# Small VectorE and GpSimd steps re-sourced, and the order of a unit's VectorE steps fixed, in a delta-rule and expert-layer kernel

## The chip, the cores and the metric

The kernel runs on one core of a Trainium2 chip. The time is that of the whole program on the device, in microseconds; the kernel before has a median of 824.09 us in three runs. In the text PE is TensorE (matmuls), PEld its weight loads, DVE is VectorE, ACT is ScalarE, POOL is GpSimd, and SP is SyncE, which issues most of the DMAs here.

## The reference

32 heads (4 batches of 8) run a delta rule over 768 steps with head size 48; the 3072 rows that come out (384 wide) go through an expert layer with a rational activation.

```python
for t in range(S):
    y[:, :, t] = einsum('bhd,bhde->bhe', q[:, :, t], state)
    v_old = einsum('bhde,bhd->bhe', state, kt)           # kt: normalized key
    state = state + bt * einsum('bhd,bhe->bhde', kt, vt - v_old)
...
h = x @ w_in                                             # 384 -> 2048
P = a[0] + a[1] * h + a[2] * h**2 + a[3] * h**3
Q = 1.0 + abs(b[0]) * abs(h) + abs(b[1]) * h**2
out = (P / (Q + 1e-06)) @ w_out                          # 2048 -> 384
```

## The kernel before, in words

The 768 steps are cut into 12 chunks of 64. Within a chunk the recurrence becomes matrix work: a Gram matrix of the keys (`pg`, line 565), the inverse of a triangular system (`inverse`, lines 574 to 642, small VectorE steps on 128x256 numbers), four rounds of solving (`solve_start`, `solve_step`, `solved`: tiles `pu` and `z`), the next state (`S`, line 763), its split (`sh`, line 726) and the outputs `y`. Each chunk of outputs is 256 rows, transposed into `xT` (line 808), and the expert layer takes them in 8 units of 256 hidden columns. So there are 96 units; unit n belongs to chunk n // 8. Numbers are kept as two float16 halves, high and low, and a product is three matmul passes; `split16` (line 238) makes the halves, the high one on ACT or POOL, the low one on DVE or POOL.

One unit has five parts. `hidden` is 18 matmuls into PSUM (`ph`, two buffers). `numerator` has the three DVE steps that read `ph`, called the PSUM steps here: line 859 (u = ph u), line 861 (w = (z + B0) ph) and line 863 (u = (u + A1) ph), behind two ACT steps (lines 856 and 858), with a third ACT step in between (line 862). `quotient` takes 1/Q by a logarithm and an exponential on ACT (lines 874 and 875), and then the DVE steps that read two SBUF tiles: the high half g (line 880, or 878), the product back (line 881) and the remainder (line 885); POOL makes the low half (line 886). In chunks 2 to 10 the units 0, 4, 5 and 6 of a chunk give the addition of A0 (line 867) and the remainder (line 883) to POOL as well (`by_pool`). `accumulate` is 12 matmuls into `po`, of which only the last four read the low half. The tiles u, r and w (`mu`, `mr`, `mw`) have three buffers each.

The loop over n writes numerator(n), quotient(n-1), a slice of the attention work of later chunks, accumulate(n-2) and hidden(n+1). That is the order of the program text only: the order on each engine is made at build time by a list scheduler, by readiness in its own model of the engines and by priorities (the solves stand at raised priority). An engine then executes its list in order, so an instruction that waits holds up all behind it. `tc.issue_after(x)` puts what is written in its block behind x in the list of x's engine; it is an order, not a wait for a result.

At the start the weights, which arrive as 64-bit floats, are made into 32-bit ones by `to_f32` (line 377): 56 blocks, each a DMA of word pairs, an ACT step on the high words (line 384), a POOL step that leaves the sign (line 385) and two DVE steps that put the bits together (line 387).

Of the kernel before, what the change touches and what calls it, by code (L numbers as in the profile page):

```python
# [37 lines left out]
def kernel(  # L38
# [338 lines left out]
    def to_f32(t, src, nm, bias=BIAS):  # L377

        n = t.shape[-1]
        st = staged([P, n, 2], U32, "ws" + nm)  # L380
        nc.sync.dma_start(out=st.rearrange("p f w -> p (f w)"), in_=src)
        wl, wh = st[..., 0], st[..., 1]
        a = sb.tile([P, n], F32, tag="mg", name="wa" + nm, bufs=MB)
        nc.scalar.activation(a, wh.bitcast(F32), AF.Abs, scale=bias)
        nc.gpsimd.tensor_scalar(t.bitcast(F32), wh.bitcast(F32), 0.0, 0.0, op0=ALU.min, op1=ALU.mult)
        for word, scalar, op0 in ((wl, 29, ALU.logical_shift_right), (a.bitcast(U32), 3, ALU.logical_shift_left)):
            nc.vector.scalar_tensor_tensor(out=t, in0=word, scalar=scalar, in1=t, op0=op0, op1=ALU.bitwise_or)

# [172 lines left out]
    def key_products(c):  # L561
        d = info[c]
        gd = d["gd"] = dpool.tile([P, BS], F32, tag="gd", name=f"gd_{c}")
        pg = bank(ps_f, f"pg_{c}", C)
        mm3(pg, d["kbd"], d.pop("tk"))
        g = sb.tile([P, HP, C], F32, tag="g", name=f"g_{c}", bufs=1)
        nc.scalar.mul(by_pair(g), pg[2], -1.0)
        for b in range(2):
            nc.sync.dma_start(out=as_rows(gd, b), in_=g[b * C : (b + 1) * C])
        gl = sb.tile([P, HP, C - 16, 2], F16, tag="gl", name=f"gl_{c}", bufs=1)  # L570
        split16([gl[..., i] for i in range(2)], g[:, :, : C - 16], eng=nc.gpsimd, hi=nc.gpsimd)
        d["gl"] = gl

    def inverse(c):


        d = info[c]
        gb = sb.tile([P, 272], F32, tag="gb", name=f"gb_{c}", bufs=1)
        dma = nc.sync.dma_start(out=gb[:, :256].rearrange("p (i j) -> p i j", j=16), in_=as_blocks(d.pop("gd")))
# [12 lines left out]

        w4 = blocks(wt, 4, 0, 68)
        a4 = xt.rearrange("p (e i j) -> p e i j", e=4, i=4)
        b4 = bblk[:, c].rearrange("p (e i) -> p e i", e=4)
        nc.vector.tensor_mul(a4, blocks(gb, 4, 0, 68), b4.unsqueeze(3).broadcast_to([P, 4, 4, 4]))
        for i in range(1, 4):
            pv = pr[:, : 4 * i * i].rearrange("p (e k j) -> p e k j", e=4, k=i)
            ai = a4[:, :, i, :i].unsqueeze(2).broadcast_to([P, 4, i, i])
            nc.vector.tensor_mul(pv, w4[:, :, :i, :i], ai)  # L600
            nc.vector.tensor_reduce(w4[:, :, :i, i], pv, axis=AX.X, op=ALU.add)

        for n in (4, 8):
            x = 34 * n
            e = 8 // n
            shape = [P, n, n, n]
            w21 = blocks(wt, n, n, x)
            prod = pr[:, : e * n ** 3].rearrange("p (e a b j) -> p e a b j", e=e, a=n, b=n)
            xs = xt[:, : e * n * n].rearrange("p (e i j) -> p e i j", e=e, i=n)
            g21, w11, w22 = blocks(gb, n, 16 * n, x), blocks(wt, n, 0, x), blocks(wt, n, 17 * n, x)  # L610
            for m in range(e):
                nc.vector.tensor_mul(
                    prod[:, m], g21[:, m].unsqueeze(1).broadcast_to(shape), w11[:, m].unsqueeze(2).broadcast_to(shape)
                )
# [12 lines left out]
        wh = sb.tile([P, 256, 2], F16, tag="wh", name=f"wh_{c}", bufs=1)
        nc.vector.tensor_scalar_mul(wh[..., 0], wtf, 256.0)
        nc.vector.scalar_tensor_tensor(
            out=wh[..., 1], in0=wtf, scalar=256.0, in1=wh[..., 0], op0=ALU.mult, op1=ALU.subtract  # L630
        )
        if c == 0:
            nc.vector.tensor_scalar(
                gate.bitcast(U32), wtf[:, 127:128].bitcast(U32), 0, 15 << 23, op0=ALU.bitwise_and, op1=ALU.bitwise_or
            )
        im = img[c % NIMG]
        words = wh.rearrange("p x i -> p (x i)").bitcast(F32)
        nc.sync.dma_start(out=as_blocks(im), in_=words.rearrange("m (t c) -> m t c", c=16))
        wc = d["wc"] = sb.tile([P, HP, C, 2], F16, tag="wc", name=f"wc_{c}", bufs=1)
        words = wc.rearrange("p m s i -> p (m s i)").bitcast(F32).rearrange("p (m s) -> p m s", s=C)  # L640
        for b in range(2):
            nc.sync.dma_start(out=words[b * C : (b + 1) * C], in_=as_rows(im, b))
# [138 lines left out]
    def tokens(c):  # L781
        yt = ys.pop(c)
        pool = ps_c if c < 3 else ps_f
        x = sb.tile([P, 2, NCC, TG], F16, tag="xT", name=f"xT_{c}")
        xs = sb.tile([P, 2], F32, tag="xs", name=f"xs_{c}")
        xm, fs = (xs[:, i : i + 1] for i in range(2))
        hot = sb.tile([P, 1], BF16, tag="hx", name=f"hx_{c}")
        sf = sb.tile([P, 6], F32, tag="sf", name=f"sf_{c}", bufs=3)
        sx = sf[:, 2:3]

        sum_squares(fs, yt.rearrange("p a e -> p (a e)"), x[:, 0].rearrange("p c t -> p (c t)"))
        px = pool.tile([P, NPAIR * 512], F32, tag="a", name=f"px_{c}")
# [12 lines left out]
        for p in PAIRS:
            for cc in range(NCC):
                nc.tensor.transpose(px[:, cc, p * P : (p + 1) * P], yt[:, p, cc * P : (cc + 1) * P], identf)
        split16(parts(x), px, sx)
        toks[c] = {"x": x, "sf": sf, "hot": hot, "ikap": {}}

    def scalars(c, lo, hi):

# [36 lines left out]
    def numerator(n):  # L849
# [6 lines left out]
        nc.scalar.activation(u, ph, AF.Identity, scale=A3, bias=a2)  # L856
        r = z = sb.tile([P, 2, TG], F32, tag="mr", name=f"mr{n}", bufs=MB)
        nc.scalar.activation(z, ph, AF.Abs, scale=B1)  # L858
        nc.vector.tensor_mul(u, ph, u)  # L859
        w = sb.tile([P, 2, TG], F32, tag="mw", name=f"mw{n}", bufs=MB)  # L860
        nc.vector.scalar_tensor_tensor(out=w, in0=z, scalar=B0, in1=ph, op0=ALU.add, op1=ALU.mult)  # L861
        nc.scalar.activation(w, w, AF.Abs)  # L862
        nc.vector.scalar_tensor_tensor(out=u, in0=u, scalar=A1, in1=ph, op0=ALU.add, op1=ALU.mult)  # L863
# [6 lines left out]
    def quotient(n):  # L870
# [3 lines left out]
        nc.scalar.activation(r, w, AF.Ln, bias=Q0)  # L874
        nc.scalar.activation(r, r, AF.Exp, scale=-1.0)  # L875
        g = sb.tile([P, 2, 2, TG], F16, tag="mg", name=f"mg{n}", bufs=MB)
        if by_pool:
            nc.vector.tensor_mul(g[:, 0], u, r)  # L878
        else:
            nc.vector.scalar_tensor_tensor(out=g[:, 0], in0=u, scalar=A0, in1=r, op0=ALU.add, op1=ALU.mult)  # L880
        nc.vector.scalar_tensor_tensor(out=w, in0=w, scalar=Q0, in1=g[:, 0], op0=ALU.add, op1=ALU.mult)  # L881
        if by_pool:
            nc.gpsimd.tensor_sub(u, u, w)  # L883
        else:
            nc.vector.scalar_tensor_tensor(out=u, in0=u, scalar=A0, in1=w, op0=ALU.add, op1=ALU.subtract)  # L885
        nc.gpsimd.tensor_mul(g[:, 1], u, r)  # L886
        d["g"] = g

# [38 lines left out]
    def back(c, j):  # L927
# [19 lines left out]
            outputs(c)  # L947
        elif j == 6:
            tokens(c)
        elif j == 7:  # L950
            if c > 0:
                scalars(c, 0, NU)

    def front(c, j):

# [123 lines left out]
```

## Time and profile before

| | |
|---|---|
| median of 3 runs (lowest, highest) | 824.09 us (821.0, 824.83) |
| the profiled execution: its time, its span | 823.32 us, 821.6 us |
| mean granted TensorE clock in it | 0.946 |
| first PSUM step of unit 0, of unit 48 | 140.7 us, 468.5 us |

The span runs from the first to the last instruction; 1.7 us of the execution lie around it. A group's row gives line, engine, operation, tiles written and read, shapes and count, then the busy time in us, the mean in ns, and the idle time ahead of it with what ended it. Durations on DVE include about 60 ns in which the next instruction already runs, so their sum is a little over the engine's busy time.

### The profile page before, as it was taken

To read this page: it belongs to the slowest core of one execution; us is meant where nothing else is said; L and a number is where in the kernel's file an instruction comes from. 1 tells how busy PE (TensorE), PEld (TensorE's weight loads), DVE (VectorE), ACT (ScalarE), POOL (GpSimd) and SP (SyncE) were. 2 spreads that over 40 slices of the span, in tenths; PEclk is the share of its full clock that TensorE was granted. 3 is DMA by queue.
4 is the path that set the end of the run, shared out by engine and by line. 5 is a ranking of instruction groups with operands and counts; after the bars stand their busy time and mean duration, and the time that the engine had idled before them with its cause. 6 is when DMAs were issued, how large, how long until landed. Compare 5 with 4: busy or idle time off the path is not lost.

```text
span 821.6 us, 23603 instructions
## 1 busy us (share of the span) xinstructions
PE 644.8 (78%) x9642; PEld 518.6 (63%) x9642; DVE 738.5 (90%) x1268; ACT 576.8 (70%) x1008; POOL 463.0 (56%) x415
## 2 busy tenths in 40 slices
PE   1321456688988889898897888988989988999995
PEld 0211355567766767776685776776777866887663
DVE  4898888798899999799899889898999799998996
ACT  3767767567867776778678578668578746877773
POOL 8987965534553473746835736635846446353532
PEclk9999856888999999999999999998999999999999
DMA  8988755728655666674565365554473632400000
GB/s 229 214 197 212 163 105 100 129 43 157 97 92 102 116 97 121 104 141 88 105 129 92 64 124 86 98 109 85 74 136 55 116 57 57 78 2 21 2 20 19
DMA packets 361100, 82.91 MB, mean 101 GB/s; under 512 B 350496, under 2 KB 357664, under 8 KB 360992
## 3 DMA queue, kind: packets, MB, share of 16 engines
q1 hardware_dynamic: 358816, 80.25, 51.6%
q8 instruction: 75, 1.23, 0.6%
q10 hardware_dynamic: 2176, 1.17, 0.5%
q14 instruction: 33, 0.27, 0.1%
HBM read 34.70 MB, written 13.65 MB: 59 GB/s over the span
## 4 chain that ended last, share of the span: by engine, by line
DVE 41%; PE 22%; DMA 10%; issue 8%; ACT 8%; POOL 6%; SPq 3%; POOLq 0%; DVEq 0%; ACTq 0%
PE ph L839 7%; PE po L901 6%; DVE mw L881 4%; DVE mu L859 4%; DVE mw L861 4%; DVE mu L863 4%; DVE mg L880 3%; DVE mu L885 3%; DVE mg L878 2%; DVE z L249 2%; PE pu L463 2%; POOL mg L886 2%; PE py L463 2%; DMA gb<-gd 2%; DMA gd<-g 2%
## 5 line engine op out<-in xcount | busy, mean ns | idle before, releaser
L901 PE MATMUL po<-w_out,mg 128*128 128x384 f16 x1152 | 216.9, 332 | 30.3 <-POOL mg L886 26.4
L839 PE MATMUL ph<-xT,w_in 128*128 128x256 f16 x1728 | 217.7, 278 | 9.3 <-DVE mu L863 9.2
L886 POOL TENSOR_TENSOR mg<-mu,mr 128x512 f16<-128x512 f32 x96 | 137.9, 1437 | 144.4 <-DVE mu L885 79.9
L839 PEld LDWEIGHTS <-w_in 128*128 128x128 f16 x1728 | 168.2, 100 | 41.4 <-DVE mu L863 9.9
L901 PEld LDWEIGHTS <-mg 128*128 128x128 f16 x1152 | 108.1, 100 | 101.1 <-POOL mg L886 34.6
L862 ACT ACTIVATE mw<-mw 128x512 f32<-128x512 f32 x96 | 60.5, 630 | 56.7 <-DVE mw L861 56.6
L856 ACT ACTIVATE mu<-ph,coef,msc 128x512 f32<-128x512 f32 x96 | 73.9, 769 | 23.6 <-PE ph L839 11.8
L881 DVE SCALAR_TENSOR_TENSOR mw<-mw,msc,mg 128x512 f32<-128x512 f32 x96 | 86.4, 900 | 0.6
L883 POOL TENSOR_TENSOR mu<-mu,mw 128x512 f32<-128x512 f32 x36 | 48.1, 1335 | 58.1 <-DVE mw L881 31.4
L859 DVE TENSOR_TENSOR mu<-ph,mu 128x512 f32<-128x512 f32 x96 | 65.3, 680 | 13.1 <-ACT mr L858 9.0
L463 PEld LDWEIGHTS <-kbd 96*128 96x128 f16 x1680 | 60.2, 103 | 18.9 <-issue 13.0
L861 DVE SCALAR_TENSOR_TENSOR mw<-mr,msc,ph 128x512 f32<-128x512 f32 x96 | 70.5, 735 | 0.0
L863 DVE SCALAR_TENSOR_TENSOR mu<-mu,msc,ph 128x512 f32<-128x512 f32 x96 | 70.5, 734 | 0.0
L874 ACT ACTIVATE mr<-mw,msc 128x512 f32<-128x512 f32 x96 | 69.0, 719 | 1.1
L858 ACT ACTIVATE mr<-ph,msc 128x512 f32<-128x512 f32 x96 | 65.1, 679 | 2.1 <-DVE w_out L249 2.1
L463 PE MATMUL pu<-z,ebd 128*128 128x48 f16 x1728 | 53.5, 187 | 13.5 <-DVE z L249 12.7
L463 PEld LDWEIGHTS <-ebd 128*128 128x128 f16 x1728 | 52.4, 99 | 16.2 <-issue 14.5
L875 ACT ACTIVATE mr<-mr 128x512 f32<-128x512 f32 x96 | 60.4, 629 | 1.2
L463 PEld LDWEIGHTS <-wbd 128*128 128x128 f16 x1152 | 34.8, 100 | 39.9 <-issue 31.9
L880 DVE SCALAR_TENSOR_TENSOR mg<-mu,msc,mr 128x512 f16<-128x512 f32 x60 | 55.7, 928 | 1.7 <-ACT mr L875 1.6
L885 DVE SCALAR_TENSOR_TENSOR mu<-mu,msc,mw 128x512 f32<-128x512 f32 x60 | 52.9, 882 | 0.4
L867 POOL TENSOR_SCALAR mu<-mu,msc 128x512 f32<-128x512 f32 x36 | 29.8, 828 | 40.6 <-DVE mu L863 40.0
(210 smaller groups left out, 1328.9 us busy)
## 6 DMA issues: line engine op xcount, KB each, us to landing
wsi<-in_moe_w_in_dram SPq DMA_DIRECT2D x24, 256.0 KB, 4.7
gd<-g SPq DMA_DIRECT2D x24, 256.0 KB, 4.2
wso<-in_moe_w_out_dram SPq DMA_DIRECT2D x32, 192.0 KB, 4.2
mbd<-mm SPq DMA_DIRECT2D x24, 256.0 KB, 4.5
wc<-img SPq DMA_DIRECT2D x24, 256.0 KB, 4.8
wbd<-wc SPq DMA_DIRECT2D x24, 256.0 KB, 4.0
k<-in_k_dram SPq DMA_DIRECT2D x48, 96.0 KB, 3.8
q<-in_q_dram SPq DMA_DIRECT2D x48, 96.0 KB, 3.4
```

Of the source, the lines that this page charges most:

```text
L463: nc.tensor.matmul(dst[p][:out, h], head(bd, lp, p * H + h)[:rows], head(rt, rp, p * H + h)[:rows], start=start and n == 0 and h == 0, sto ...
L839: nc.tensor.matmul(ph[:, i], w_in[:, f2, wp, cc, i * P : (i + 1) * P], x[:, xp, cc], start=k == 0, stop=k == 3 * NCC - 1,)
L856: nc.scalar.activation(u, ph, AF.Identity, scale=A3, bias=a2)
L859: nc.vector.tensor_mul(u, ph, u)
L861: nc.vector.scalar_tensor_tensor(out=w, in0=z, scalar=B0, in1=ph, op0=ALU.add, op1=ALU.mult)
L863: nc.vector.scalar_tensor_tensor(out=u, in0=u, scalar=A1, in1=ph, op0=ALU.add, op1=ALU.mult)
L874: nc.scalar.activation(r, w, AF.Ln, bias=Q0)
L880: nc.vector.scalar_tensor_tensor(out=g[:, 0], in0=u, scalar=A0, in1=r, op0=ALU.add, op1=ALU.mult)
L881: nc.vector.scalar_tensor_tensor(out=w, in0=w, scalar=Q0, in1=g[:, 0], op0=ALU.add, op1=ALU.mult)
L885: nc.vector.scalar_tensor_tensor(out=u, in0=u, scalar=A0, in1=w, op0=ALU.add, op1=ALU.subtract)
L886: nc.gpsimd.tensor_mul(g[:, 1], u, r)
L901: nc.tensor.matmul(po[p], g[:, gp, i, p * P : (p + 1) * P], w_out[:, f2, wp, i], start=f2 == lo and i == 0 and k == 0, stop=f2 == hi - 1 a ...
```

## The change

Five edits. (1) In `to_f32` ACT keeps the sign (Copy for Abs) and POOL takes the sign from ACT's dense result `a`, where it read every second word of the DMA's tile. (2) The split of the Gram matrix `gl` leaves POOL: its high half is made by ACT and its low half by DVE, both from PSUM (`pg`). (3) The high half `wh` of the inverse goes from DVE to ACT. (4) For chunks after the first, the scalars of a chunk (`msc`) are multiplied from PSUM in `tokens`, where `scalars` did it from an SBUF copy one slice later. (5) The PSUM steps of unit n are listed behind the last DVE step of quotient(n-2), and quotient(n-1) behind the PSUM steps of unit n. The line numbers of the quotient move by 6 (886, 887, 891 for 880, 881, 885; 884 for 878; 892 for 886), those of the PSUM steps by 5.

```diff
@@ to_f32
-        nc.scalar.activation(a, wh.bitcast(F32), AF.Abs, scale=bias)
-        nc.gpsimd.tensor_scalar(t.bitcast(F32), wh.bitcast(F32), 0.0, 0.0, op0=ALU.min, op1=ALU.mult)
+        nc.scalar.activation(a, wh.bitcast(F32), AF.Copy, scale=bias)
+        nc.gpsimd.tensor_scalar(t.bitcast(F32), a, 0.0, 0.0, op0=ALU.min, op1=ALU.mult)
@@ key_products
-        split16([gl[..., i] for i in range(2)], g[:, :, : C - 16], eng=nc.gpsimd, hi=nc.gpsimd)
+        split16([by_pair(gl[..., i]) for i in range(2)], pg[2][..., : C - 16], -1.0)
@@ inverse
-        nc.vector.tensor_scalar_mul(wh[..., 0], wtf, 256.0)
+        nc.scalar.activation(wh[..., 0], wtf, AF.Copy, scale=256.0)
@@ tokens
+        m = None
         if c > 0:
             looked_up(pl, hot, t_x[:, 1])
             nc.scalar.copy(sf, pl)
+            m = sb.tile([P, 6, NU], F32, tag="msc", name=f"msc_{c}")
+            nc.vector.tensor_mul(m, tab, pl.unsqueeze(2).broadcast_to([P, 6, NU]))
...
-        toks[c] = {"x": x, "sf": sf, "hot": hot, "ikap": {}}
+        toks[c] = {"x": x, "sf": sf, "hot": hot, "m": m, "ikap": {0: (NU, sf[:, 1:2])} if c > 0 else {}}
@@ numerator
-        nc.vector.tensor_mul(u, ph, u)
+        with nullcontext() if last["rem"] is None else tc.issue_after(last["rem"]):
+            nc.vector.tensor_mul(u, ph, u)
...
-        nc.vector.scalar_tensor_tensor(out=u, in0=u, scalar=A1, in1=ph, op0=ALU.add, op1=ALU.mult)
+        last["psum"] = nc.vector.scalar_tensor_tensor(out=u, in0=u, scalar=A1, in1=ph, op0=ALU.add, op1=ALU.mult).ins
@@ quotient
+        with tc.issue_after(last["psum"]):
+            if by_pool:
+                nc.vector.tensor_mul(g[:, 0], u, r)
+            else:
+                nc.vector.scalar_tensor_tensor(out=g[:, 0], in0=u, scalar=A0, in1=r, op0=ALU.add, op1=ALU.mult)
+        last["rem"] = nc.vector.scalar_tensor_tensor(out=w, in0=w, scalar=Q0, in1=g[:, 0], op0=ALU.add, op1=ALU.mult).ins
...
+            last["rem"] = nc.vector.scalar_tensor_tensor(out=u, in0=u, scalar=A0, in1=w, op0=ALU.add, op1=ALU.subtract).ins
@@ back
-        elif j == 7:
-            if c > 0:
-                scalars(c, 0, NU)
```

What it does to the lists is shown at three places. First VectorE around unit 36, before (mu36 is tile u of unit 36, `z_6_0` a solve, `m32_7` and `wt0` attention work):

```order
L859 TENSOR_TENSOR mu36_7505<-ph_36_7486,mu36_7505 128x512
L861 SCALAR_TENSOR_TENSOR mw36_7510<-mr36_7507,msc_4_6472,ph_36_7486 128x512
L881 SCALAR_TENSOR_TENSOR mw35_7396<-mw35_7396,msc_4_6472,mg35_7517 128x512
L713 TENSOR_TENSOR m32_7_7102<-pm_7_7053,mask_91 128x1024
L622 TENSOR_REDUCE wt0_125<-pr_7_7037 128x8x8
L863 SCALAR_TENSOR_TENSOR mu36_7505<-mu36_7505,msc_4_6472,ph_36_7486 128x512
L249 SCALAR_TENSOR_TENSOR z_6_0_7750<-pu_6_7645,zmask_85,z_6_0_7750 128x768
L885 SCALAR_TENSOR_TENSOR mu35_7391<-mu35_7391,msc_4_6472,mw35_7396 128x512
L628 TENSOR_SCALAR wh_7_7351<-wt0_125 128x256
L629 SCALAR_TENSOR_TENSOR wh_7_7351<-wt0_125,wh_7_7351 128x256
L859 TENSOR_TENSOR mu37_7573<-ph_37_7554,mu37_7573 128x512
```

The same place on VectorE after:

```order
L864 TENSOR_TENSOR mu36_7505<-ph_36_7486,mu36_7505 128x512
L866 SCALAR_TENSOR_TENSOR mw36_7510<-mr36_7507,msc_4_6416,ph_36_7486 128x512
L249 SCALAR_TENSOR_TENSOR et_6_7028<-pe_6_6977,et_6_7028 128x768
L615 TENSOR_REDUCE ab_7_7038<-pr_7_7037 128x64
L868 SCALAR_TENSOR_TENSOR mu36_7505<-mu36_7505,msc_4_6416,ph_36_7486 128x512
L886 SCALAR_TENSOR_TENSOR mg35_7517<-mu35_7391,msc_4_6416,mr35_7393 128x512
L617 TENSOR_TENSOR pr_7_7037<-ab_7_7038,wt0_125 128x512
L887 SCALAR_TENSOR_TENSOR mw35_7396<-mw35_7396,msc_4_6416,mg35_7517 128x512
L713 TENSOR_TENSOR m32_7_7102<-pm_7_7053,mask_91 128x1024
L622 TENSOR_REDUCE wt0_125<-pr_7_7037 128x8x8
L891 SCALAR_TENSOR_TENSOR mu35_7391<-mu35_7391,msc_4_6416,mw35_7396 128x512
L864 TENSOR_TENSOR mu37_7573<-ph_37_7554,mu37_7573 128x512
```

Before, the steps of quotient 35 stood among the PSUM steps of unit 36; now all of them stand behind these, with nothing of unit 37 among them.

Second, VectorE at the boundary between the chunks 5 and 6 (unit 48 is the first of chunk 6; `z_7`, `S16` and `sh_8` are the solve, the state and its split of later chunks), before:

```order
L247 TENSOR_TENSOR z_7_9431<-pu_7_8763,z_7_9431 128x768
L881 SCALAR_TENSOR_TENSOR mw47_8857<-mw47_8857,msc_5_7590,mg47_9019 128x512
L885 SCALAR_TENSOR_TENSOR mu47_8852<-mu47_8852,msc_5_7590,mw47_8857 128x512
L763 SCALAR_TENSOR_TENSOR S16_147<-pd_7_9434,sc_7_6856,S16_147 96x768
L249 SCALAR_TENSOR_TENSOR sh_8_9643<-S16_147,sc_8_7974,sh_8_9643 96x768
L271 TENSOR_SCALAR kq_9_9083<-pfq_9_9085 128x2
L859 TENSOR_TENSOR mu48_9007<-ph_48_8988,mu48_9007 128x512
```

The same boundary after, from the solve to the quotient of unit 47:

```order
L247 TENSOR_TENSOR z_7_9431<-pu_7_8763,z_7_9431 128x768
L887 SCALAR_TENSOR_TENSOR mw46_8751<-mw46_8751,msc_5_7534,mg46_8863 128x512
L249 SCALAR_TENSOR_TENSOR xT_6_8640<-px_6_8645,sf_6_8643,xT_6_8640 128x768
L763 SCALAR_TENSOR_TENSOR S16_147<-pd_7_9434,sc_7_6856,S16_147 96x768
L249 SCALAR_TENSOR_TENSOR gl_9_8973<-pg_9_8920,gl_9_8973 128x768
L249 SCALAR_TENSOR_TENSOR sh_8_9643<-S16_147,sc_8_7974,sh_8_9643 96x768
L864 TENSOR_TENSOR mu48_9007<-ph_48_8988,mu48_9007 128x512
L866 SCALAR_TENSOR_TENSOR mw48_9012<-mr48_9009,msc_6_8652,ph_48_8988 128x512
L868 SCALAR_TENSOR_TENSOR mu48_9007<-mu48_9007,msc_6_8652,ph_48_8988 128x512
L886 SCALAR_TENSOR_TENSOR mg47_9019<-mu47_8852,msc_5_7534,mr47_8854 128x512
```

Quotient 47 stood ahead of the state step and now stands behind the PSUM steps of unit 48; the low half `gl_9` has come in between the state and its split.

Third, POOL at the boundary of the chunks 3 and 4, before:

```order
L886 TENSOR_TENSOR mg31_6783<-mu31_6616,mr31_6618 128x512
L241 TENSOR_SCALAR gl_7_6737<-g_7_6733 128x768
L247 TENSOR_TENSOR gl_7_6737<-g_7_6733,gl_7_6737 128x768
L867 TENSOR_SCALAR mu32_6771<-mu32_6771,msc_4_6472 128x512
L883 TENSOR_TENSOR mu32_6771<-mu32_6771,mw32_6776 128x512
L886 TENSOR_TENSOR mg32_6921<-mu32_6771,mr32_6773 128x512
```

And POOL there after:

```order
L892 TENSOR_TENSOR mg31_6783<-mu31_6616,mr31_6618 128x512
L889 TENSOR_TENSOR mu32_6771<-mu32_6771,mw32_6776 128x512
L892 TENSOR_TENSOR mg32_6921<-mu32_6771,mr32_6773 128x512
L892 TENSOR_TENSOR mg33_7190<-mu33_6910,mr33_6912 128x512
L892 TENSOR_TENSOR mg34_7402<-mu34_7179,mr34_7181 128x512
```

The two `gl` steps are gone from POOL, and the addition for unit 32 now stands ahead of these rows.

More of the change, by code (lines that the diff above doesn't have):

```diff
@@ L824, in scalars @@
         d["ikap"][lo] = hi, sf[:, 1:2]
+    last = {"psum": None, "rem": None}
     unit = {}
@@ L876, in quotient @@
         g = sb.tile([P, 2, 2, TG], F16, tag="mg", name=f"mg{n}", bufs=MB)
[L877 to L881, printed above, removed]
+        with tc.issue_after(last["psum"]):
[4 more added lines that the diff above has]
+        last["rem"] = nc.vector.scalar_tensor_tensor(out=w, in0=w, scalar=Q0, in1=g[:, 0], op0=ALU.add, op1=ALU.mult).ins
         if by_pool:
@@ L884, in quotient @@
         else:
-            nc.vector.scalar_tensor_tensor(out=u, in0=u, scalar=A0, in1=w, op0=ALU.add, op1=ALU.subtract)
+            last["rem"] = nc.vector.scalar_tensor_tensor(out=u, in0=u, scalar=A0, in1=w, op0=ALU.add, op1=ALU.subtract).ins
         nc.gpsimd.tensor_mul(g[:, 1], u, r)
```

## The prediction

> **What bounds the kernel now.** I read the busy times first, then the chain that ended last, two windows, and the groups of instructions with single steps out of the order of time. Of the page, the span, the busy times and the chain's shares:
>
> ```profile
> span 821.6 us, 23603 instructions
> PE 644.8 (78%) x9642; PEld 518.6 (63%) x9642; DVE 738.5 (90%) x1268; ACT 576.8 (70%) x1008; POOL 463.0 (56%) x415
> DVE 41%; PE 22%; DMA 10%; issue 8%; ACT 8%; POOL 6%; SPq 3%; POOLq 0%; DVEq 0%; ACTq 0%
> ```
>
> DVE is busy for 90% and carries 41% of the chain, PE 22%. The windows (us; busy time of PE, PEld, DVE, ACT, POOL; PE clock; DMA share) compare the setup with the middle, chunks that are alike:
>
> ```profile
> 0.00:160.00 160.00, 63.43 (x938) 53.77 (x938) 132.61 (x320) 107.33 (x250) 124.02 (x145) 0.86 0.76 169
> 280.00:700.00 420.00, 373.24 (x5944) 302.76 (x5942) 386.73 (x590) 300.34 (x484) 236.53 (x189) 0.97 0.55 97
> ```
>
> In the middle DVE is idle for 33.3 of 420 us and PE for 46.8: what DVE gives up shows in the time, but PE is close behind. In the setup DVE and POOL are both busy, PE is not. Part of DVE's busy time is no work. Single steps (start, length):
>
> ```profile
> 500.29 2.37 POOL L247 TENSOR_TENSOR mm<-m,mm 128x1024 f16<-128x1024 f32 x1 [0.26 <-ACT mm L243]
> 501.02 2.19 DVE L878 TENSOR_TENSOR mg<-mu,mr 128x512 f16<-128x512 f32 x1
> 726.02 0.68 DVE L878 TENSOR_TENSOR mg<-mu,mr 128x512 f16<-128x512 f32 x1
> ```
>
> The same DVE step takes 0.68 us alone, and 2.19 beside a POOL step that ends at 502.66; DVE ends at 503.21, 0.55 later. A DVE step with two SBUF tiles stands still while POOL runs. The groups show whom this hits (busy us, mean ns, idle time before):
>
> ```profile
> L881 DVE SCALAR_TENSOR_TENSOR mw<-mw,msc,mg 128x512 f32<-128x512 f32 x96 | 86.4, 900 | 0.6
> L880 DVE SCALAR_TENSOR_TENSOR mg<-mu,msc,mr 128x512 f16<-128x512 f32 x60 | 55.7, 928 | 1.7 <-ACT mr L875 1.6
> L885 DVE SCALAR_TENSOR_TENSOR mu<-mu,msc,mw 128x512 f32<-128x512 f32 x60 | 52.9, 882 | 0.4
> L878 DVE TENSOR_TENSOR mg<-mu,mr 128x512 f16<-128x512 f32 x36 | 32.3, 899 | 0.0
> L861 DVE SCALAR_TENSOR_TENSOR mw<-mr,msc,ph 128x512 f32<-128x512 f32 x96 | 70.5, 735 | 0.0
> L859 DVE TENSOR_TENSOR mu<-ph,mu 128x512 f32<-128x512 f32 x96 | 65.3, 680 | 13.1 <-ACT mr L858 9.0 <-issue 1.7 <-POOL mg L886 1.0
> L886 POOL TENSOR_TENSOR mg<-mu,mr 128x512 f16<-128x512 f32 x96 | 137.9, 1437 | 144.4 <-DVE mu L885 79.9 <-ACT mw L862 17.4 <-ACT ob L915 12.8
> L883 POOL TENSOR_TENSOR mu<-mu,mw 128x512 f32<-128x512 f32 x36 | 48.1, 1335 | 58.1 <-DVE mw L881 31.4 <-DVE wt L601 11.0 <-DVE pr L600 7.4
> ```
>
> The PSUM steps (859, 861) are not stretched: 680 and 735 ns. Against these the quotient loses 96x(900-735) = 15.8, 60x(928-735) = 11.6, 60x(882-735) = 8.8 and 36x(899-680) = 7.9 us, in sum 44.1.
>
> **The change part by part**, in us of DVE's path unless said otherwise.
>
> *(5) The order.* After it, the three PSUM steps of the next unit, 680+735+735 ns = 2.15 us, stand between the last DVE step of a quotient and the next quotient. POOL's low half (1.44) of a unit without `by_pool` (60 of 96) falls under them and stretches nothing. With `by_pool` POOL has 1.34+1.44 = 2.77 behind the product back, more than 2.15, and POOL's attention steps (the 2.37 above) come when they come. So I take half of the 44.1: -22, between 0 (the blocking falls on other steps) and -35. The order also delays a quotient by up to those 2.15 us. Behind it wait POOL's low half and PE's accumulate:
>
> ```profile
> L901 PE MATMUL po<-w_out,mg 128*128 128x384 f16 x1152 | 216.9, 332 | 30.3 <-POOL mg L886 26.4 <-DVE mg L878 3.5
> ```
>
> PE waits 26.4 us for that half now. I cost the delay at nothing within a chunk, since PE has `hidden` of the next unit and attention work ahead of the next accumulate; if that cover is gone, PE's waits of 26.4 grow, which is part of the slower rival.
>
> *(1) The loads.*
>
> ```profile
> L385 POOL TENSOR_SCALAR w_out<-wso 128x192 f32<-128x192 f32 x28 | 27.6, 1003 | 8.1 <-DMA wso<-in_moe_w_out_dram 8.0
> L385 POOL TENSOR_SCALAR w_out<-wsi 128x256 f32<-128x256 f32 x24 | 27.3, 1158 | 1.0 <-DMA wsi<-in_moe_w_in_dram 0.9
> L387 DVE SCALAR_TENSOR_TENSOR w_out<-wso,w_out 128x192 uint32<-128x192 uint32 x28 | 13.2, 477 | 0.0
> L387 DVE SCALAR_TENSOR_TENSOR w_out<-wsi,w_out 128x256 uint32<-128x256 uint32 x24 | 13.1, 549 | 5.7 <-POOL w_out L385 5.7
> 62.67 0.41 DVE L387 SCALAR_TENSOR_TENSOR w_out<-wai,w_out 128x256 uint32<-128x256 uint32 x1
> 77.52 0.35 DVE L387 SCALAR_TENSOR_TENSOR w_out<-wao,w_out 128x192 uint32<-128x192 uint32 x1
> L384 ACT ACTIVATE wai<-wsi 128x256 f32<-128x256 f32 x24 | 10.0, 426 | 2.0 <-DVE w_out L387 1.8
> L867 POOL TENSOR_SCALAR mu<-mu,msc 128x512 f32<-128x512 f32 x36 | 29.8, 828 | 40.6 <-DVE mu L863 40.0 <-DVE kq L271 0.4
> L241 POOL TENSOR_SCALAR gl<-g 128x768 f16<-128x768 f32 x12 | 13.5, 1127 | 4.8 <-ACT g L567 4.6
> ```
>
> POOL takes 1158 ns for 256 numbers at a stride, but 828 for 512 dense and 1127 for 768 dense ones. From these two, (1127-828)/256 = 1.17 ns a number, an estimate for dense reads is 0.53 us for 256 and 0.45 for 192: POOL loses 24x0.63+28x0.55 = 30 us. DVE's steps of the loads exceed the undisturbed ones by 24x(549-410)+28x(477-350) = 6.9, and DVE waited 5.7 for POOL. POOL's step now waits for ACT too (0.43), and the DMA share of 0.76 holds the first loads: I take -5, between 0 and -12.
>
> [...]
>
> *(2) The Gram split.*
>
> ```profile
> L247 POOL TENSOR_TENSOR gl<-g,gl 128x768 f16<-128x768 f32 x12 | 23.4, 1948 | 0.7
> L249 DVE SCALAR_TENSOR_TENSOR et<-pe,et 128x768 f16<-128x768 f32 x12 | 11.4, 948 | 5.3 <-ACT et L245 5.3
> L245 ACT ACTIVATE et<-pe 128x768 f16<-128x768 f32 x12 | 9.7, 805 | 10.0 <-PE pe L463 10.0
> L249 DVE SCALAR_TENSOR_TENSOR sh<-S,sc,sh 96x768 f16<-96x768 f32 x11 | 17.7, 1606 | 4.0 <-ACT sh L245 4.0
> 463.78 1.01 DVE L763 SCALAR_TENSOR_TENSOR S<-pd,sc,S 96x768 f32<-96x768 f32 x1 [1.43 <-PE pd L463]
> 465.79 2.67 DVE L249 SCALAR_TENSOR_TENSOR sh<-S,sc,sh 96x768 f16<-96x768 f32 x1 [1.00 <-ACT sh L245]
> 465.83 1.82 POOL L247 TENSOR_TENSOR gl<-g,gl 128x768 f16<-128x768 f32 x1
> 468.46 0.67 DVE L859 TENSOR_TENSOR mu<-ph,mu 128x512 f32<-128x512 f32 x1
> ```
>
> POOL is rid of 13.5+23.4 = 36.9. The same split of `et` from PSUM costs DVE 0.948: +11.4. ACT gets 12x0.805 = 9.7, hidden at 70% busy. Given back: `sh` stood behind just this POOL step (465.83 to 467.65, DVE to 468.46); by the 1.01 of line 763 in the same size, 11x(1.606-1.01) = 6.6, of which I take -5 (0 to -6.6). The `gl` DMAs of SP move with their source; nothing near waits for them.
>
> [...] The rows show no difference: line 859 with PSUM 680 ns, line 878 without 0.68 us.
>
> *(3), (4).*
>
> ```profile
> L628 DVE TENSOR_SCALAR wh<-wt 128x256 f16<-128x256 f32 x12 | 8.1, 675 | 0.0
> L823 DVE TENSOR_TENSOR msc<-tab,sf 128x48 f32<-128x48 f32 x11 | 7.0, 633 | 0.0
> L823 DVE TENSOR_TENSOR msc<-tab,sf 128x48 f32<-128x48 f32 x1 | 0.2, 194 | 0.0
> ```
>
> `wh` leaves DVE, 8.1; ACT makes it in the 0.43 of line 384, and the low half on DVE must wait for that unless other steps lie between: -7 (-2 if the wait shows, 12x0.43 = 5.2). `msc` from PSUM is not stretched: 11x(633-194) = -4.8 (the single row is one seen alone), at worst 0.
>
> *The boundary.* Ahead of unit 48, quotient 47 filled time in which the state was being made:
>
> ```profile
> 459.08 1.05 DVE L881 SCALAR_TENSOR_TENSOR mw<-mw,msc,mg 128x512 f32<-128x512 f32 x1
> 460.92 1.43 DVE L885 SCALAR_TENSOR_TENSOR mu<-mu,msc,mw 128x512 f32<-128x512 f32 x1
> ```
>
> Now it stands behind the PSUM steps of 48, and DVE has `gl` alone for the waits of 1.43 and 1.00. I take 0.8 us more idle for each of 11 chunks, +9, between 0 and +25 (2.4 each, both waits again).
>
> *Sum.* -5-22+11.4-5-7-4.8 = -32.4. Not all of it shows, since DVE idles 8% and PE has only 46.8 of 420 us left; I take 0.8, by DVE's idle share and about as much again for PE: -25.9. With +9: -16.9. The profiled execution took 823.3 us (1.7 of it around the span): 806.4. The median lies 0.8 above it: **807**.
>
> **The rivals.**
>
> *More: POOL's blocking nearly vanishes, and PE binds.* For: the whole 44.1 would give a sum of -54. Against: PE is idle for 46.8 of 420, 11%, of which the solves leave about half unavoidable. Of the 680 us of units that is about 680/420x46.8/2 = -38: 786.
>
> [...]
>
> *The change does not do it.* Lists of instructions fix an order, no time: POOL's steps may meet other two-tile DVE steps (of the inverse) or the next quotient. With -5 for (5) and nothing at loads and `sh`: -5+11.4-7-4.8 = -5.4, x0.8 = -4, with +3 at the boundary for less to lose: 823.
>
> *Slower: the boundary.* In before the three steps of a quotient, 0.93+0.90+0.88 = 2.7 and up to 3.4 with stretching, (in the rows at 459 to 461, 1.05 and 1.43 of it) stand ahead of the state's wait. If the wait stays where it is, and the quotient of the old chunk comes wholly behind it, with accumulate of that unit and the next `hidden` behind that on PE, each boundary loses 3.4: +37 against -25.9, and 823.3+11.5+0.8 is 836. For: the order shows it, and `S` waits for PE in it (the 1.43 above). Against: PE can fill in with other work, and DVE does lose none of its work. It decides from (25.9+4)/11 = 2.7 us a boundary.
>
> **How the numbers follow.** Forecast 0.50 (alone 793 to 818: with (5) between -35 and -8, x0.8, it is 797 to 818, and half of the boundary's 9 below that); PE binds 0.16; the page's rule 0.07; nothing gained 0.12; boundary 0.15. The range from 782 to 829 holds the first four and the mild end of the last. About 0.5%, 4 us, can be told from no change: faster than 820 is 0.50+0.16+0.07 = 0.73, within it 0.12, slower 0.15.
>
> **What would show it.** Right: lines 886, 887 and 891 at 740 to 830 ns for 900; the POOL step of the loads at 0.45 to 0.55 us; `sh` near 1.1; POOL busy near 395 us; DVE busy near 706; eleven waits of some 2 us ahead of `S` and `sh`. [...] If the three PSUM steps often wait ahead of a finished quotient, with DVE idle within a chunk, the order itself costs what no term above holds.

## The result, and the profile after

The changed kernel takes 829.98 us (median of 17 runs, 823.62 to 837.16), the kernel before beside it 823.35 (17 runs, 819.86 to 825.63): ratio 1.0083, 95% interval 1.0065 to 1.0101. One of the changed kernel's 17 runs, the longest, counts as a slow run and is left out of the ratio; the other 16 lie between 823.62 and 834.29. So it is slower by 0.8%, where 807 was forecast, and 1 us outside the range. The profiled execution is the fastest of the changed kernel's (823.62, its span as long as before), so its trace shows where the saving went, and only part of what the median loses.

Span, busy times and shares of the chain after:

```profile
span 821.9 us, 23556 instructions
PE 648.5 (79%) x9642; PEld 521.0 (63%) x9642; DVE 703.2 (86%) x1268; ACT 592.2 (72%) x1032; POOL 427.7 (52%) x391
DVE 36%; PE 17%; ACT 14%; DMA 12%; issue 9%; POOL 7%; SPq 3%; POOLq 0%; ACTq 0%; DVEq 0%
```

VectorE works 35.3 us less (738.5 before), close to the 32.4 of the prediction's sum, and the span is the same. The windows (us; PE, PEld, DVE, ACT, POOL; PE clock; DMA share):

```profile
0.00:160.00 160.00, 67.25 (x991) 56.82 (x992) 133.15 (x333) 114.11 (x262) 120.20 (x140) 0.89 0.80 173
280.00:700.00 420.00, 374.12 (x5966) 304.32 (x5962) 355.68 (x581) 306.48 (x490) 210.67 (x170) 0.96 0.53 94
```

In the middle VectorE's idle time went from 33.3 to 64.3 us; PE is as busy as before (374 for 373). What VectorE no longer did, it waited. The groups that answer to those of before:

```profile
L887 DVE SCALAR_TENSOR_TENSOR mw<-mw,msc,mg 128x512 f32<-128x512 f32 x96 | 80.3, 837 | 1.0
L886 DVE SCALAR_TENSOR_TENSOR mg<-mu,msc,mr 128x512 f16<-128x512 f32 x60 | 49.7, 828 | 0.0
L891 DVE SCALAR_TENSOR_TENSOR mu<-mu,msc,mw 128x512 f32<-128x512 f32 x60 | 51.0, 850 | 0.7
L884 DVE TENSOR_TENSOR mg<-mu,mr 128x512 f16<-128x512 f32 x36 | 30.9, 859 | 0.0
L249 DVE SCALAR_TENSOR_TENSOR gl<-pg,gl 128x768 f16<-128x768 f32 x12 | 12.2, 1020 | 12.6 <-ACT gl L245 12.5
L249 DVE SCALAR_TENSOR_TENSOR sh<-S,sc,sh 96x768 f16<-96x768 f32 x11 | 11.3, 1029 | 0.5 <-ACT sh L245 0.3
L803 DVE TENSOR_TENSOR msc<-tab,px 128x48 f32<-128x48 f32 x11 | 2.0, 183 | 0.0
L385 POOL TENSOR_SCALAR w_out<-wai 128x256 f32<-128x256 f32 x24 | 27.6, 1162 | 7.9 <-ACT wai L384 7.7
L385 POOL TENSOR_SCALAR w_out<-wao 128x192 f32<-128x192 f32 x28 | 26.0, 938 | 7.3 <-ACT wao L384 5.8 <-ACT lgw L291 1.2
L387 DVE SCALAR_TENSOR_TENSOR w_out<-wso,w_out 128x192 uint32<-128x192 uint32 x28 | 12.4, 442 | 0.7 <-POOL w_out L385 0.7
L387 DVE SCALAR_TENSOR_TENSOR w_out<-wsi,w_out 128x256 uint32<-128x256 uint32 x24 | 14.7, 612 | 6.8 <-POOL w_out L385 6.8
```

The quotient's steps are shorter, `sh` takes 1029 ns for 1606, and `msc` 2.0 us in all for 7.0; `gl` costs its 12.2 and waits 12.6 more, 12.5 of it for ScalarE. With a dense read the POOL step of the loads takes 1162 ns for 1158, and 938 for 1003 in the other form. VectorE's waits in the middle of the kernel (280 to 700 us), first of before, then after (us in total, times, longest):

```profile
DVE ab L596 <- DMA gb<-gd: 7.8, 5, 2.7
DVE mu L859 <- ACT mr L858: 5.2, 5, 1.9
...
DVE S L763 <- PE pd L463: 1.6, 2, 1.4
```

```profile
DVE S L763 <- PE pd L463: 15.2, 4, 4.7
DVE mu L864 <- ACT mr L862: 10.3, 9, 4.1
DVE gl L249 <- ACT gl L245: 10.0, 7, 3.7
DVE xT L249 <- ACT xT L245: 9.3, 4, 2.7
```

The first and the third stand at the boundary of two chunks. Here is the boundary of the chunks 4 and 5, in the order of time (start, length). It is the one whose rows before stand in the prediction: the step at 468.5 us is the first PSUM step of unit 40, and the quotient ahead of it that of unit 39. The table and the prediction call them 48 and 47, but unit 48 begins at 526.6 us before. At this boundary `gl` stands ahead of `S`, where the list shown for the chunks 5 and 6 has it behind:

```profile
463.24 0.95 DVE L247 TENSOR_TENSOR z<-pu,z 128x768 f16<-128x768 f32 x1
467.88 1.02 DVE L249 SCALAR_TENSOR_TENSOR gl<-pg,gl 128x768 f16<-128x768 f32 x1 [3.69 <-ACT gl L245]
468.79 1.00 DVE L763 SCALAR_TENSOR_TENSOR S<-pd,sc,S 96x768 f32<-96x768 f32 x1
471.25 0.69 DVE L864 TENSOR_TENSOR mu<-ph,mu 128x512 f32<-128x512 f32 x1 [1.46 <-ACT mr L862]
...
473.23 0.75 DVE L886 SCALAR_TENSOR_TENSOR mg<-mu,msc,mr 128x512 f16<-128x512 f32 x1
```

and the reciprocal of unit 39 on ScalarE, which that quotient (line 886) needs:

```profile
456.51 0.63 ACT L880 ACTIVATE mr<-mr 128x512 f32<-128x512 f32 x1
```

The inputs of quotient 39 are there at 457.1, and it starts at 473.2; in the rows shown VectorE does nothing for 5.2 us meanwhile. So my first theory, **A**, was the prediction's slower rival: the boundary's price. Its rivals: **B**, VectorE's saving finds no room, whatever the order; **C**, the `gl` split costs; later **D**, the lists that the scheduler makes afresh decide; and **E**, against D, that the change costs by itself on any lists.

### The profile page after: what moved, and what is told of

Its sections match the earlier page's. It is cut to its first block, busy times and chain, and to the rows that moved or that the text cites. A ratio compares the mean times of both kernels' runs of the same rounds, so it can differ in the third digit from the quotient of the medians.

```text
span 821.9 us, 23556 instructions
## 1 busy us (share of the span) xinstructions
PE 648.5 (79%) x9642; PEld 521.0 (63%) x9642; DVE 703.2 (86%) x1268; ACT 592.2 (72%) x1032; POOL 427.7 (52%) x391
## 3 DMA queue, kind: packets, MB, share of 16 engines
q10 hardware_dynamic: 2176, 1.17, 0.5%
## 4 chain that ended last, share of the span: by engine, by line
DVE 36%; PE 17%; ACT 14%; DMA 12%; issue 9%; POOL 7%; SPq 3%; POOLq 0%; ACTq 0%; DVEq 0%
PE ph L843 5%; PE po L907 5%; DVE mu L864 4%; DVE mw L866 4%; DVE mw L887 3%; DVE mu L868 3%; DVE mg L886 3%; DVE mu L891 3%; DMA gd<-g 2%; DVE w_out L387 2%; DMA gb<-gd 2%; PE pu L463 2%; PE pd L463 2%; ACT mu L860 2%; ACT mr L879 2%
## 5 line engine op out<-in xcount | busy, mean ns | idle before, releaser
L907 PE MATMUL po<-w_out,mg 128*128 128x384 f16 x1152 | 225.1, 338 | 26.5 <-POOL mg L892 20.4
L892 POOL TENSOR_TENSOR mg<-mu,mr 128x512 f16<-128x512 f32 x96 | 127.4, 1327 | 166.7 <-DVE mu L891 100.7
L872 POOL TENSOR_SCALAR mu<-mu,msc 128x512 f32<-128x512 f32 x36 | 45.2, 1256 | 69.5 <-DVE mu L868 68.7
L887 DVE SCALAR_TENSOR_TENSOR mw<-mw,msc,mg 128x512 f32<-128x512 f32 x96 | 80.3, 837 | 1.0
L864 DVE TENSOR_TENSOR mu<-ph,mu 128x512 f32<-128x512 f32 x96 | 65.5, 683 | 17.4 <-ACT mr L862 13.4
L889 POOL TENSOR_TENSOR mu<-mu,mw 128x512 f32<-128x512 f32 x36 | 45.8, 1273 | 51.6 <-DVE mw L887 21.7
L463 PEld LDWEIGHTS <-kbd 96*128 96x128 f16 x1680 | 58.8, 101 | 15.4 <-issue 11.9
L891 DVE SCALAR_TENSOR_TENSOR mu<-mu,msc,mw 128x512 f32<-128x512 f32 x60 | 51.0, 850 | 0.7
L886 DVE SCALAR_TENSOR_TENSOR mg<-mu,msc,mr 128x512 f16<-128x512 f32 x60 | 49.7, 828 | 0.0
```

Source lines behind the costliest of these rows:

```text
L463: nc.tensor.matmul(dst[p][:out, h], head(bd, lp, p * H + h)[:rows], head(rt, rp, p * H + h)[:rows], start=start and n == 0 and h == 0, sto ...
L887: last["rem"] = nc.vector.scalar_tensor_tensor(out=w, in0=w, scalar=Q0, in1=g[:, 0], op0=ALU.add, op1=ALU.mult).ins
L891: last["rem"] = nc.vector.scalar_tensor_tensor(out=u, in0=u, scalar=A0, in1=w, op0=ALU.add, op1=ALU.subtract).ins
L907: nc.tensor.matmul(po[p], g[:, gp, i, p * P : (p + 1) * P], w_out[:, f2, wp, i], start=f2 == lo and i == 0 and k == 0, stop=f2 == hi - 1 a ...
```

## The experiments: parts of the change

Four kernels on one chip (the kernel before 821.96 us there).

**edge_free**: the boundary's order is left out.

```diff
-        with nullcontext() if last["rem"] is None else tc.issue_after(last["rem"]):
+        with nullcontext() if last["rem"] is None or n % NU == 0 else tc.issue_after(last["rem"]):
...
-        with tc.issue_after(last["psum"]):
+        with nullcontext() if n % NU == NU - 1 else tc.issue_after(last["psum"]):
```

> The changed kernel without its order at the boundary of two chunks: the PSUM steps of a chunk's first unit and the quotient of the last unit of the chunk before are free of each other; all else stays. Theory A (the boundary): in the trace of the changed kernel VectorE idles 44.5 us in the unit intervals that hold the nine boundaries of chunks 2 to 10, against 15.2 before, while units within a chunk come 2.06 us a chunk sooner; given the quotient back as cover, 29 us of idle become 10 to 15, and the time is 805 to 817. Theory B (VectorE's saving has no place to show, whatever the order, since the solves and ACT wait as long): 824 to 832, the waits only move.

Measured: 834.81 us, 1.0150 (1.0122 to 1.0178). A and B both missed, A by 18 us. The wait that A speaks of did go:

```profile
L763 DVE SCALAR_TENSOR_TENSOR S<-pd,sc,S 96x768 f32<-96x768 f32 x10 | 10.0, 1004 | 0.8 <-PE pd L463 0.8
```

(15.4 us of idle time ahead of it in the changed kernel), and the time did not follow. VectorE's busy time rose from 703.2 to 720.0 at the same steps.

**edge_only**: the kernel before with just that order (`n % NU` and `n % NU != NU - 1` as the conditions).

> The kernel before with the new order at the chunk boundaries alone; no other part of the change. Theory A: the boundary's waits come without the gains, each of 11 boundaries some 2 us longer: 838 to 850. Theory B: same as before, within 5 us of 823.

Measured: 844.03, 1.0252 (1.0224 to 1.0281), as A said. Together with edge_free that looked like a contradiction: the order at the boundary costs 22 us where it is put in, and nothing comes back where it is taken out.

**all_but_order**: the changed kernel without (5).

```diff
-        with nullcontext() if last["rem"] is None else tc.issue_after(last["rem"]):
+        with nullcontext():
...
-        with tc.issue_after(last["psum"]):
+        with nullcontext():
```

> The changed kernel with the four re-sourced steps and without any of the order (5). Theory A: the terms that were measured in the changed kernel (gl on VectorE +12.2, sh -6.4, wh -8.1 with the wait hidden, msc -5, loads about 0) sum to -7, so 815 to 822. Theory C (the gl split on VectorE and ACT is what costs, since it now waits for ACT within the chain of the chunk): 826 to 834.

Measured: 824.50, 1.0030 (1.0009 to 1.0050): between A and C.

**order_only**: the kernel before with (5), and none of (1) to (4).

> The kernel before with the order (5) alone, everywhere. Theory A: within chunks some -19, at the boundaries some +20 and more, as gl does not stand there to fill: 822 to 832. Theory C: without the gl split the order gains: 805 to 815.

Measured: 828.95, 1.0080 (1.0052 to 1.0109): inside A's range, C falls.

What follows: no sum of parts gives these five times. By order_only and edge_only the order within chunks would be worth 15 us, so edge_free, which has it without the boundary's order, should take some 809; it took 834.81. What the five share is that each change of a step or an order makes the scheduler write all five engines' lists anew. Hence D; I call each such writing of the lists a draw.

## The experiments: the lists held

A kernel's lists can be held by an edge from each instruction to the next on its engine, an order and no wait:

```diff
+        for a, b in zip(rank, rank[1:]):
+            tc.add_manual_dep(own[int(b)], own[int(a)].name, DependencyInfo(NoSync, DATA), reason="pinned")
```

`rank` is a table of one engine's list. (2) to (4) were made from chunk 2 on, so that the setup stayed as it was (`if c < 2:` with the old step at the three places).

**edits_late**: with lists made afresh.

> The kernel before with the edits (2), (3), (4) from chunk 2 on, and its lists made afresh by the scheduler; the setup, the loads and the order are as before. Theory D (the scheduler makes new lists for all engines whenever a step changes, and these lists, not the steps, lose what the steps save): 822 to 832, though VectorE's busy time falls by some 6 us (gl +10, sh -5, wh -7, msc -4.5) and GpSimd's by 31. Theory B (there is no room, whatever the lists): 821 to 826. Theory C (the steps gain by themselves): 812 to 818.

**lists_of_before**: the same steps, lists held to those of the kernel before.

> The same instructions as in edits_late, but each engine's list is held to that of the kernel before, by an edge from each instruction to the next; only the steps that changed engines are put in (gl behind the Gram matrix on ScalarE and about 1.1 us later on VectorE, wh where its source is ready, msc behind the copy of the scalars). Theory D: the saving of 6 us on VectorE and the missing GpSimd steps show: 812 to 819. Theory B: 821 to 826, the same as edits_late.

**dve_inner**: the kernel before, all lists held, and on VectorE's the order (5) within the chunks.

> The kernel before, its lists held on every engine, and on VectorE's list alone the order (5) imposed for the units 17 to 95 except the first of each chunk; no step changes. Theory D with A: the blocking of the quotient falls by some 15 us and the boundaries stay as they are: 803 to 815. Theory B: 820 to 828, VectorE's busy time falls and its idle time rises by as much.

**lists_of_before_inner**: both.

> lists_of_before with the order (5) on VectorE's list for the units 17 to 95 except the first of each chunk. Theory D with A: both savings together: 795 to 810, faster than both kernels. Theory B: 820 to 828.

Measured, on one chip (before 822.97):

| kernel | us | ratio (95%) |
|---|---|---|
| edits_late | 854.71 | 1.0372 (1.0330 to 1.0414) |
| lists_of_before | 824.46 | 1.0009 (0.9983 to 1.0036) |
| dve_inner | 835.68 | 1.0143 (1.0099 to 1.0186) |
| lists_of_before_inner | 836.18 | 1.0148 (1.0110 to 1.0185) |

The first two run the same steps, 30 us apart; the fourth shows again that the steps add nothing to the third. The busy times, of edits_late and then of lists_of_before:

```profile
PE 658.3 (77%) x9642; PEld 525.1 (61%) x9642; DVE 737.3 (86%) x1268; ACT 591.0 (69%) x1028; POOL 440.2 (51%) x395
```

```profile
PE 643.8 (78%) x9642; PEld 518.2 (63%) x9642; DVE 738.0 (90%) x1268; ACT 588.2 (72%) x1028; POOL 433.2 (53%) x395
```

VectorE works equally long in both; the difference is waiting, among others in the solves and at the state. PE works 14.5 us longer on the same matmuls in edits_late, at a granted clock of 0.932 for 0.956. That the clock sets the time is unlikely: the kernel before took 822.97 us at 0.902 on that chip, and 824.14 at 0.971. Groups of edits_late, then of lists_of_before (the last column is the idle time ahead):

```profile
L912 PE MATMUL po<-w_out,mg 128*128 128x384 f16 x1152 | 225.0, 342 | 36.0 <-POOL mg L897 31.4 <-DVE mg L891 1.9 <-DVE xs L271 1.3
L249 DVE SCALAR_TENSOR_TENSOR z<-pu,zmask,z 128x768 f16<-128x768 f32 x36 | 36.4, 1011 | 7.6 <-ACT z L245 7.5
L769 DVE SCALAR_TENSOR_TENSOR S<-pd,sc,S 96x768 f32<-96x768 f32 x10 | 10.0, 997 | 10.6 <-PE pd L463 10.5
```

```profile
L912 PE MATMUL po<-w_out,mg 128*128 128x384 f16 x1152 | 214.4, 330 | 23.7 <-POOL mg L897 20.4 <-DVE mg L889 2.3 <-DVE mg L891 0.8
L249 DVE SCALAR_TENSOR_TENSOR z<-pu,zmask,z 128x768 f16<-128x768 f32 x36 | 36.2, 1006 | 2.2 <-ACT z L245 1.8
L769 DVE SCALAR_TENSOR_TENSOR S<-pd,sc,S 96x768 f32<-96x768 f32 x10 | 10.1, 1008 | 2.8 <-PE pd L463 2.8
...
L249 DVE SCALAR_TENSOR_TENSOR sh<-S,sc,sh 96x768 f16<-96x768 f32 x11 | 16.2, 1477 | 2.2 <-ACT sh L245 2.1
```

So D has the sense of edits_late right and its size wrong: the time lies 23 us over D's range, and VectorE's busy time fell by 1 us, not by 6. D's other half falls: with the lists held, the steps gain nothing (B's number, though B has it for both kernels). GpSimd is rid of 30 us, yet VectorE's busy time stays at 738, since `gl` adds 10.2 and `sh` still takes 1477 ns (1606 before): it took 1029 in the changed kernel, so an estimate is that it now stands beside other POOL steps.

dve_inner lies outside both ranges, and so does lists_of_before_inner. B's reason doesn't hold either: VectorE's busy time did not fall (740.2; from 280 to 700 us it is 387.8 for 386.7). The quotient's four groups fell by 3.4 us only (to 223.9), and `wh` on line 628 rose from 8.1 to 11.8 (984 ns for 675). In the trace of before this step took 0.30 us at 503.13, with no POOL step running, and 1.55 at 675.48, beside a POOL step of 2.65; an estimate from these is that the blocking fell on it instead. And PE shows a new wait.

```profile
L901 PE MATMUL po<-w_out,mg 128*128 128x384 f16 x1152 | 217.6, 330 | 47.8 <-POOL mg L886 19.8 <-DVE mg L880 16.9 <-DVE mg L878 10.7
```

PE's accumulate waits 27.6 us for the high half of the quotient, 3.5 before: where PE's list stays, a quotient behind the next unit's PSUM steps comes too late for it. In the changed kernel PE's list was made for the late quotient, and this wait is 3.9:

```profile
L907 PE MATMUL po<-w_out,mg 128*128 128x384 f16 x1152 | 225.1, 338 | 26.5 <-POOL mg L892 20.4 <-DVE mg L886 2.5 <-DVE mg L884 1.4
```

In none of the kernels with held lists did VectorE's work shrink (738.0, 740.2 and 740.6 for 738.5; from 280 to 700 us 387.7, 387.8 and 385.6 for 386.7). So what a real saving on VectorE would be worth with the lists held is not tested.

Not tried: the changed kernel's lists held, with only the quotient at the boundary moved ahead on VectorE. So what the boundary costs by itself stays open here.

## The experiments: the same steps, other lists

The raised priority of the solves (300, at nine places) changes no step, only the lists:

```diff
-            with tc.high_priority(300):
+            with tc.high_priority(290):
```

**before_p290, after_p290, before_p400, after_p400**: kernel before and changed kernel with 290 and 400.

> The kernel before, step for step, with the raised priority of the solves set to 290 for 300, which makes the scheduler write other lists; nothing else. Theory D (what decides is which lists come out, and those of the kernel before are a good draw): over 828, and the idle time of VectorE grows while its busy time stays within 5 us. Theory E (the change costs by itself, lists made afresh are as good as any): 820 to 827.

> The changed kernel with the same priority 290. Theory D: anywhere between 815 and 845, and as likely below before_p290 as above it. Theory E: 5 to 10 us above before_p290.

> The kernel before with the priority 400, a third draw of its lists. Theory D: over 828. Theory E: 820 to 827.

> The changed kernel with the priority 400. Theory D: 815 to 845, of either sign against before_p400. Theory E: 5 to 10 us above before_p400.

**edge_free_p290, edge_free_p400, all_but_order_p290, all_but_order_p400**: the kernels above with these priorities.

> The changed kernel with the boundary's order freed and the priority 290. Theory A (the boundary has a price of its own, and edge_free at 834.8 was a bad draw): below after_p290 by 5 to 15, so 812 to 822. Theory D alone (no price of its own that stands out of the draws): either sign, 815 to 840.

> The same with the priority 400. Theory A: below after_p400, so 803 to 813. Theory D alone: either sign, 810 to 840.

> The changed kernel without the order (5), priority 290. If the order (5) costs by itself: below after_p290, 815 to 823. If it gains by itself: above after_p290, 830 to 840. Theory D alone: either.

> The changed kernel without the order (5), priority 400. If the order costs by itself: 805 to 815. If it gains by itself: 822 to 840. Theory D alone: either.

**before_p250, after_p250**: a fourth pair.

> The kernel before with the priority 250, a fourth draw. If the list of the kernel before at 300 is one of the better draws: over 826. Otherwise 815 to 825.

> The changed kernel with the priority 250. If the change gains on an average draw (mean of the three pairs so far 831 before, 825 changed): 815 to 830, and below before_p250. If it does not: above before_p250.

Measured, medians in us (the kernel before ran beside each at 821 to 824.3, so that some 3 us may be the chip's):

| steps | 300 | 290 | 400 | 250 | mean of the first three |
|---|---|---|---|---|---|
| before | 823.35 | 827.84 | 841.63 | 832.10 | 830.9 |
| changed | 829.98 | 827.38 | 817.33 | 832.05 | 824.9 |
| changed, boundary free | 834.81 | 822.01 | 828.64 | | 828.5 |
| changed, without (5) | 824.50 | 848.58 | 860.25 | | 844.4 |

- The same steps differ by 18 us before and 15 changed, by the lists alone. The kernel before is the best of its four draws. At 290 both theories miss it by less than 1 us (827.84, between E's 827 and D's 828; the ratio to before, 1.0067, from 1.0042 to 1.0091, is clear of no change). At 400 D holds and E does not. E's price of the change falls, since the pairs differ by +6.6, -0.5, -24.3 and 0.0, mean -4.5. Four settings of one priority are no sample at random, so the mean says little.
- The boundary: freeing it gives +4.8, -5.4, +11.3. A's forecast came true at 290 (5 to 15 below after_p290; it was 5.4) and failed at 300 and 400; a price of its own does not stand out of the draws. Nor does VectorE's idle time there set the time: summed over the ten boundaries of the chunks 1 to 11 in each trace (from the first PSUM step of a chunk's last unit to that of the next chunk's first) it is 16 us before and 50 changed, and freeing takes it from 50 to 31, from 51 to 17 and from 42 to 23 at 300, 290 and 400, while the time rises in two of the three.
- The order as a whole: without it the changed kernel is 5.5 faster at 300, then 21 and 43 slower, further than either expectation. In lists made afresh it has no fixed price; in three draws the lists with it are nearer together and better (817 to 830) than those without (825 to 860).
- The fourth pair came out equal: before_p250 as expected (over 826), after_p250 neither below it nor above, so whether the change gains on an average draw stays undecided.
- after_p400 beats both kernels: ratio to the kernel before 0.9922 (0.9895 to 0.9948).

VectorE's saving is in every draw (24 to 39 us in the four pairs), whatever the time. Busy times of before_p400, then of after_p400:

```profile
PE 654.4 (78%) x9642; PEld 525.7 (63%) x9642; DVE 747.2 (89%) x1268; ACT 578.2 (69%) x1008; POOL 459.8 (55%) x415
```

```profile
PE 644.3 (79%) x9642; PEld 519.3 (64%) x9642; DVE 708.1 (87%) x1268; ACT 589.5 (72%) x1032; POOL 415.1 (51%) x391
```

and of after_p250, at 832 us:

```profile
PE 652.4 (78%) x9642; PEld 521.5 (63%) x9642; DVE 710.1 (85%) x1268; ACT 592.5 (71%) x1032; POOL 430.9 (52%) x391
```

Two programs with 708 and 710 us of work on VectorE take 817 and 832.

## Why the prediction was wrong

**The sum of VectorE's work came out close by luck**: -32.4 forecast, -35.3 measured, but its own terms measure -21.9. Term by term:

| term | forecast | measured |
|---|---|---|
| (5) the quotient's four groups | -22 | -15.4 (211.9 for 227.3) |
| (1) line 387, the two groups shown | -5 | +0.8 (27.1 for 26.3) |
| (2) `gl` on VectorE | +11.4 | +12.2 |
| (2) given back at `sh` | -5 | -6.4 |
| (3) `wh` | -7 | -8.1, no wait |
| (4) `msc` | -4.8 | -5.0 |

The other 13.4 of the 35.3 came from steps that no term named: among them the small products of the inverse (line 600). Their median is 172 ns before and 176 after, but the longest, beside POOL steps, took 2343 before and 381 after. Before and after:

```profile
L600 DVE TENSOR_TENSOR pr<-wt,ab 128x4 f32<-128x4 f32 (+2 forms) x36 | 13.0, 361 | 0.4
```

```profile
L600 DVE TENSOR_TENSOR pr<-wt,ab 128x4 f32<-128x4 f32 (+2 forms) x36 | 6.9, 192 | 0.0
```

**(1) was wrong in kind.** The dense read took 1162 ns for 1158 at a stride, and 938 for 1003 in the other form, so the outcome that was given 0.07, no gain at the loads, came true on this term, though not on the time. The estimate of 1.17 ns a number came from steps with other operations; that the operation makes the difference is not tested.

**The step that failed is the 0.8, and the boundary's +9 with it.** The prediction let 80% of VectorE's saving show, because it idled only 8% of the time; with the +9 it forecast 15.5 us more idle time on VectorE (6.5 and 9). Measured in the profiled execution are 35.6 us more (83.1 before, 118.7 after, the span less the busy time), which is all that was saved; 31.0 of them stand in the middle. The step took for granted that the waits between the engines stay while VectorE's work shrinks, and they did not. What moved them is shown in part. The same steps in other lists take up to 36 us more (the changed kernel without (5) at 300 and 400), so lists made anew are enough to do it; but they are not the whole: in lists that are held, the order alone cost 1.4% (dve_inner), and removing 30 us from POOL and exchanging steps on VectorE changed nothing (1.0009). That the changed kernel lost its saving by its new lists, and not by the order as such, is not shown.

**The delay of the quotient, costed at nothing**, was named with its price ("if that cover is gone, PE's waits of 26.4 grow"). Where PE's list stays (dve_inner) its waits ahead of accumulate rose from 30.3 to 47.8 us; in the changed kernel they are 26.5, as PE's list moved along.

**The boundary, +9**: the mechanism was seen rightly and is larger. The state step, before and after:

```profile
L763 DVE SCALAR_TENSOR_TENSOR S<-pd,sc,S 96x768 f32<-96x768 f32 x10 | 10.0, 1001 | 1.7 <-PE pd L463 1.6
```

```profile
L763 DVE SCALAR_TENSOR_TENSOR S<-pd,sc,S 96x768 f32<-96x768 f32 x10 | 10.1, 1009 | 15.4 <-PE pd L463 15.4
```

It waits 15.4 us for 1.7, `gl` waits 12.6, and `sh` 0.5 for 4.0: together some 23 more over 11 boundaries, 2.1 each, the upper end of what was given (0 to 25). The slower rival (836, from 2.7 a boundary) missed the median by 6 us. That the boundary is the cause is not shown: the wait at `S` went away in edge_free, and the time rose.

**Nothing gained** (823, 7 us off) was the other rival near the result; its reason (the blocking moves elsewhere) is wrong for the changed kernel, as the quotient's steps did get shorter, though the groups of dve_inner agree with it (the four 3.4 us less, `wh` 3.7 more).

What is settled: the change shortens VectorE's work in each of its four draws, and over these the sign of its gain changes with the lists. What stays open: which property of a list makes it good; whether the change gains on an average list (mean -4.5 over four pairs that differ by +7 to -24); and why the changed kernel's own 16 runs spread over 10.7 us, those of before over 5.8.

## What to carry to other kernels

Where a scheduler writes the lists, a change of steps is two changes: the steps, and a new draw of the lists. Measure the spread of draws first (a priority moved by a little, no step changed), hold the lists to see what the steps are worth, and only then forecast a gain that is smaller than the spread, or take the best of a few draws of the changed kernel, as after_p400 shows. A saving on an engine that is 92% busy, as here, is not yet a saving of time: what it waits for on the other engines has to be counted too.

## What the runs showed of the hardware

In the traces of before and after VectorE and GpSimd lengthen each other's steps, both ways. POOL's addition for the units with `by_pool` (828 ns before) became much longer after the change. The quotient's two-tile steps now stand right beside it: 35 of the 36 additions begin while one of them runs (median 1.12 us), 8 of 36 before (1.06; the other 28 have a median of 0.69):

```profile
L872 POOL TENSOR_SCALAR mu<-mu,msc 128x512 f32<-128x512 f32 x36 | 45.2, 1256 | 69.5 <-DVE mu L868 68.7
```

In the order of time, first VectorE and then POOL, and last the same POOL step undisturbed:

```profile
569.60 0.68 DVE L884 TENSOR_TENSOR mg<-mu,mr 128x512 f16<-128x512 f32 x1
```

```profile
569.78 1.07 POOL L872 TENSOR_SCALAR mu<-mu,msc 128x512 f32<-128x512 f32 x1 [0.17 <-DVE mu L868]
```

```profile
331.44 0.68 POOL L872 TENSOR_SCALAR mu<-mu,msc 128x512 f32<-128x512 f32 x1
```

VectorE starts first and ends at 570.28; POOL ends at 570.85, 0.57 later, as VectorE ended 0.55 behind POOL in the prediction's row. The other way round, 94 two-tile steps of the quotient begin in the trace of before while a POOL step runs: 76 of them end 0.48 to 0.57 behind it (median length 1.18 us), 7 end well ahead of it at 0.68 to 0.74 us, so the prediction's sentence on such steps holds for most and not for all. So a step moved away from the blocking on one engine may bring it to the other: 15.4 us more on POOL here, which is busy for 52% of the span.
